# Weight gradient of a strided convolution: stored sums of the second batch's input rows, three more split leaves, and a new written order

## The chip, the cores and the metric

The kernel runs on one core of a Trainium2 chip. The metric is the time of the program on the device in microseconds (us). The engines are called by their short names in the profile: PE is TensorE with its matmuls, PEld its weight loads, DVE VectorE, ACT ScalarE, POOL GpSimd and SP SyncE, the engine from whose queue nearly all DMAs are issued. Engines run side by side, each works through its own instructions in the order written, and they wait for each other by semaphores.

## The reference

The reference is a convolution over time with 31 taps, stride 2 and 256 channels in and out, on two sequences (batches) of 16000 rows, then a normalisation over the whole time axis for each channel, scale and shift, and a tanh-approximated GELU. The function returns the output and the gradients to all four inputs.

```python
def _fwd_reference(x, w, gn_gamma, gn_beta):      # x (2,16000,256)  w (31,256,256), bfloat16
    s, L = 2, (T - K) // 2 + 1                    # L = 7985
    h = sum(einsum('blc,cd->bld', x[:, i:i + s*L:s, :], w[i]) for i in range(K))
    mu = h.sum(1) / L;  var = ((h - mu)**2).sum(1) / L
    return gelu((h - mu) / sqrt(var + 1e-5) * gn_gamma + gn_beta)
def reference(x, w, gn_gamma, gn_beta, grad_out):
    out, vjp = jax.vjp(_fwd_reference, x, w, gn_gamma, gn_beta)
    return (out, *vjp(grad_out))                  # out, dx, dw, dgamma, dbeta
```

## The kernel before, in words

The program has three large pieces of matmul work: the forward convolution (stages F0 and F1), the gradient to x (G0 for batch 0 up to its last chunk, G1 from there on), and the gradient to w (W). In all three a nested scheme of sums replaces four products by three: rows or taps are grouped in pairs, and a product of a pair is made from the three combinations "first", "second" and "both", called A, C_ and B_. In W the scheme has three levels. The outer two give nine combinations n = 0 to 8, listed in COMBOS as (i1, i2):

```python
COMBOS = ((A, A), (A, C_), (A, B_), (C_, B_), (B_, B_), (B_, A), (B_, C_), (C_, A), (C_, C_))
```

**A combination n of W.** weight_grad() goes through the nine of them. For each it needs two tiles of x rows per batch (`xt[b, 0]` and `xt[b, 1]`, 128 x 4096 elements, 1 MB each), their sum `XSUM[b]`, and rows of the incoming gradient, which the input gradient has left in DRAM as nine tensors dl_d per batch. Where B_ stands in a combination, the x tile is a sum of two raw tiles. x_tile (L1325) makes it: for batch 0 it loads a finished sum from the DRAM tensor xs_d; for batch 1 it loads two raw tiles and adds them on DVE with w_add (L1316). Where B_ stands in both places it adds two tiles that are there. XSUM is one more w_add for each batch (L1507), except for batch 0 in combinations 6 and 7, where it is loaded from xss_d.

Within a combination there are three products, worked in two halves h of 256 input channels and kept in PSUM pairs X[h] and Y[h]. The one of the sums (pm) goes first: pair_x (L1417 or L1421) and pair_d (L1437) make sums and differences on DVE, w_pairs multiplies them, w_single multiplies the singles. Then come leaf A into Y and leaf C_ into X, both on top of what pm left. A leaf is either whole (w_leaf: for each half and each batch 16 matmuls with 512 columns) or split once more, if (n, leaf) stands in NODES. A split leaf has pair_x, two pair_d, w_pairs with 16 matmuls of 256 columns for each half, w_both (L1461), which adds the kept product of pm to PSUM on DVE, and w_single with 32 matmuls of 256 columns for each half. So w_single waits for w_both, and w_both for w_pairs. leaf_d (L1520 for n = 0, L1525 after) makes the leaf's gradient rows DL. Results are kept by ACT (L585), added by DVE (L581), or added and sent out by w_emit (L1380).

```python
NODES = {(6, C_), (5, A), (0, A), (0, C_), (1, A), (2, A), (3, A), (4, A), (6, A), (7, A), (7, C_), (8, C_)}
```

**The stored sums of batch 0.** x_sums(f) (L750), called eight times in the forward pass of batch 0, loads 1 MB of raw rows into XA, makes the three sums with three adds on DVE (L754 twice, L758 once), and stores them to xs_d (two DMAs) and xss_d (one). Eight such calls cover a batch.

**The input gradient.** input_grad() goes over batch b, chunk c = 0 to 3, half chunk pr = 0 and 1, and the three branches br in the order B_, A, C_. One (b, c, pr) is called a turn here; it ends with a store of 1 MB to out_1 out of the tile HO. Results of branches A and C_ are put into HO by ACT (L585) and corrected by a DVE add (L1213), or, in chunks 0 to 2 of batch 0, by one DVE add (L1217). HO has two buffers of 8192 bytes per partition: chunks 0 to 2 of batch 0 use only HO[0], all later turns alternate with pr. ACT also copies shared products for TensorE (g_copy, L1165). dl_turn transposes gradient rows by DMA and POOL stores them to dl_d. The next chunk's gradient tiles are loaded by SP (e_load).

**Memory.** Nearly all tiles lie at fixed offsets in one arena per partition, and tiles of different stages overlap. HO[1] lies at bytes 144128 to 152320; the tiles DL of the stage W begin at 146880. HO[0] lies at 119232 to 127424, and a buffer for a split leaf of n = 0 at 110720 to 127104.

**Order.** Every operation is first put in a list with its reads and writes; an operation in it is one instruction, or for TensorE a group of usually 8 or 16 matmuls. The list SEQUENCE, a written permutation of the operations' numbers, then fixes the order in which all are emitted; each engine keeps that order, and SP's DMA queue too.

## Time and profile before

| | |
|---|---|
| timed runs | 1113.3, 1113.68 and 1115.04 us; median 1113.68 us |
| the profiled execution, first to last instruction | 1111.2 us (the page gives no other time of it) |
| PE busy | 1086.2 us, 98% |
| weight loads busy | 749.8 us, 67% |
| DVE busy | 919.9 us, 83% |
| ACT busy | 578.9 us, 52% |
| POOL busy | 129.3 us, 12% |
| DMA moved | 256.16 MB, mean 231 GB/s |

The stages follow each other on TensorE: forward until about 407 us, input gradient from there to about 801 us, weight gradient to 1106 us; the rest is the last store. A busy share over the whole span mixes these stages, so the stretches are looked at one by one. In a row of stretches each engine's busy time stands in us with its count of instructions in brackets; the DMA share is the time that packets took, over 16 DMA engines, and can pass 1. In a row of waits stand the total, the number of times and the longest.

### The profile page before, as it was taken

How to read it: one execution, taken by the hardware profiler on the slowest of the kernel's cores; microseconds unless marked ns; L12 is line 12 of the kernel's file. 1: busy time of each engine (PE TensorE's matmuls, PEld its weight loads, DVE VectorE, ACT ScalarE, POOL GpSimd, SP SyncE). 2: the span in 40 equal slices, each digit the busy share in tenths (PEclk: the TensorE clock that was granted, in tenths of full speed). 3: DMA queues.
4: the chain of work that ended last, by engine and by line, in shares of the span. 5: the costliest groups of instructions: out<-in, count | busy, mean ns of one | idle time of the engine just before them, and what ended most of it. 6: DMA issues, size and time to landing. Idle time of an engine off the chain costs nothing.

```text
span 1111.2 us, 18967 instructions
## 1 busy us (share of the span) xinstructions
PE 1086.2 (98%) x7623; PEld 749.8 (67%) x7672; DVE 919.9 (83%) x900; ACT 578.9 (52%) x880; POOL 129.3 (12%) x233
## 2 busy tenths in 40 slices
PE   6999999999999989999999999999999999999998
PEld 4888899878787974444444444444587776678885
DVE  7987877889999999989897565644789699699995
ACT  1234434587988569899964566545413322111221
POOL 0000000000001003232332432251200000000000
PEclk9999999999999999999999999999999999999999
DMA  9979899876969789999999898577994959978888
GB/s 231 198 188 249 233 275 267 219 167 162 209 166 219 240 328 270 274 252 265 217 225 237 179 203 183 157 201 197 278 293 137 270 156 298 303 254 279 282 253 207
DMA packets 348806, 256.16 MB, mean 231 GB/s; under 512 B 234327, under 2 KB 315869, under 8 KB 343517
## 3 DMA queue, kind: packets, MB, share of 16 engines
q1 hardware_dynamic: 341613, 236.05, 81.8%
q0 software_dynamic: 7104, 18.89, 6.3%
q8 instruction: 60, 0.98, 0.4%
q14 instruction: 29, 0.24, 0.1%
HBM read 114.62 MB, written 84.45 MB: 179 GB/s over the span
## 4 chain that ended last, share of the span: by engine, by line
PE 89%; DVE 5%; issue 2%; DMA 1%; SPq 1%; ACT 1%; DVEq 0%
PE ps L1136 34%; PE ps L506 34%; PE ps L1351 21%; SPq L314 1%; DMA out_dram<-arena 1%; DVE arena L1437 1%; DVE ps L1461 1%; DMA arena<-in_w_dram 1%; DVE arena L1421 1%; DVE arena L1380 1%; DVE arena L1525 0%; DVE arena L581 0%; DVE arena L1417 0%; DVE arena L448 0%; DVE arena L1316 0%
## 5 line engine op out<-in xcount | busy, mean ns | idle before, releaser
L506 PE MATMUL ps<-arena 128*128 128x256 bf16 (+4 forms) x3464 | 396.6, 278 | 11.2 <-DMA arena<-in_x_dram 4.7
L1136 PE MATMUL ps<-arena 128*128 128x512 bf16 (+1 forms) x1787 | 388.1, 376 | 5.7 <-ACT ps L1165 3.6
L506 PEld LDWEIGHTS <-arena 128*128 128x128 bf16 x3464 | 338.2, 98 | 69.4 <-DMA arena<-in_x_dram 5.8
L1136 PEld LDWEIGHTS <-arena 128*128 128x128 bf16 x1824 | 178.5, 98 | 215.1 <-issue 2.9
L1351 PE MATMUL ps<-arena 128*128 128x256 bf16 (+1 forms) x2372 | 301.6, 289 | 3.4 <-DVE arena L1520 1.8
L1351 PEld LDWEIGHTS <-arena 128*128 128x128 bf16 x2384 | 233.2, 98 | 71.9 <-issue 2.3
L585 ACT ACTIVATE arena<-ps 128x1024 bf16<-128x1024 f32 (+1 forms) x121 | 122.1, 1022 | 213.0 <-PE ps L1351 77.3
L464 DVE TENSOR_TENSOR arena<-arena 128x2064 bf16<-128x2064 bf16 (+7 forms) x131 | 162.7, 1265 | 24.2 <-PE ps L506 23.0
L314 POOL DMA_DIRECT2D dld<-arena x144 | 104.6, 728 | 246.7 <-DMA arena<-arena 229.4
L1199 DVE TENSOR_TENSOR ps<-ps,arena 128x1024 f32<-128x1024 f32 x36 | 44.3, 1232 | 64.2 <-PE ps L1136 53.2
L1082 DVE TENSOR_TENSOR arena<-arena 128x1032 bf16<-128x1032 bf16 (+1 forms) x114 | 89.5, 813 | 9.5 <-POOL arena L1049 4.3
L551 ACT ACTIVATE ps<-ps 128x256 f32<-128x256 f32 x89 | 36.7, 412 | 85.6 <-PE ps L506 84.5
L1316 DVE TENSOR_TENSOR arena<-arena 128x4096 bf16<-128x4096 bf16 x30 | 68.3, 2287 | 0.5 <-DMA arena<-in_x_dram 0.3
L1165 ACT COPY ps<-ps 128x512 f32<-128x512 f32 x84 | 48.1, 575 | 33.7 <-PE ps L1136 30.0
L323 POOL MEMSET arena<- 128x104 bf16 (+11 forms) x52 | 12.0, 249 | 414.8 <-DVE arena L464 157.6
L923 DVE TENSOR_TENSOR arena<-arena 128x2048 bf16<-128x2048 bf16 (+1 forms) x48 | 57.5, 1197 | 3.0 <-ACT arena L926 1.3
L605 ACT ACTIVATE arena<-ps 128x512 bf16<-128x512 f32 (+1 forms) x64 | 37.0, 582 | 32.7 <-PE ps L506 28.2
L885 DVE TENSOR_TENSOR arena<-arena 128x2048 bf16<-128x2048 bf16 (+1 forms) x40 | 47.7, 1197 | 4.0 <-ACT arena L879 1.7
L1437 DVE TENSOR_TENSOR arena<-arena 128x2048 bf16<-128x2048 bf16 x40 | 48.5, 1220 | 2.4 <-PE ps L1351 2.4
L1461 DVE TENSOR_TENSOR ps<-ps,arena 128x1024 f32<-128x1024 f32 x24 | 29.1, 1227 | 19.5 <-PE ps L1351 19.5
L1453 ACT COPY ps<-ps 128x256 f32<-128x256 f32 x54 | 19.0, 360 | 47.8 <-PE ps L1351 46.7
L1525 DVE TENSOR_TENSOR arena<-arena 128x4608 bf16<-128x4608 bf16 x16 | 40.6, 2554 | 0.0
(92 smaller groups left out, 752.3 us busy)
## 6 DMA issues: line engine op xcount, KB each, us to landing
arena<-in_x_dram SPq DMA_DIRECT2D x36, 1024.0 KB
arena<-hd SPq DMA_DIRECT2D x40, 512.0 KB
dld<-arena POOLq DMA_DIRECT2D x144, 128.0 KB, 4.4
out_dram<-arena SPq DMA_DIRECT2D x14, 1024.0 KB
arena<-dld SPq DMA_DIRECT2D x18, 640.0 KB
arena<-dld SPq DMA_DIRECT2D x18, 576.0 KB
vl<-arena SPq DMA_DIRECT2D x36, 256.0 KB
arena<-vl SPq DMA_DIRECT2D x9, 1024.0 KB
```

The lines of the kernel that those rows point to most:

```text
L314: lambda: e.dma_start(out=out, in_=in_), dma=np_ * ns / 16e3 * 1.03, ns=ns, tp=SH[pk], slack=slack)
L464: lambda: nc.vector.tensor_tensor(out=o, in0=a, in1=b, op=ALU.add))
L506: yield nc.tensor.matmul(ps[:, dh, cs], lhsT=wt, rhs=mv, start=s0, stop=False, skip_group_check=True)
L585: lambda: nc.scalar.activation(out=out, in_=ps, func=ACT.Copy, scale=scale))
L885: add("DVE", dve(nf), [o], [a, b_], lambda: V.tensor_tensor(out=o, in0=a, in1=b_, op=op))
L923: add("DVE", dve(nf), [o], [a, b_], lambda: V.tensor_tensor(out=o, in0=a, in1=b_, op=op))
L1082: lambda: nc.vector.tensor_tensor(out=o, in0=a, in1=b, op=ALU.subtract))
L1136: yield nc.tensor.matmul(ps[:, e, 0:wide], lhsT=lt, rhs=mv, start=s0, stop=False, skip_group_check=True)
L1165: add("ACT", act(512), [o], [i], lambda: nc.scalar.copy(out=o, in_=i))
L1316: add("DVE", dve(4096), [o], [a, b], lambda: nc.vector.tensor_tensor(out=o, in0=a, in1=b, op=ALU.add))
L1351: yield nc.tensor.matmul(ps[:, s, c0:c1], lhsT=lt, rhs=mv, start=s0, stop=False, skip_group_check=True)
L1437: add("DVE", dve(2048), [o], [u, v], lambda o=o, u=u, v=v: nc.vector.tensor_tensor(out=o, in0=u, in1=v, op=ALU.subtract))
```

## The change

The x sums are made for batch 1 as well. x_sums gets a batch argument, xs_d and xss_d get one tensor per batch, and the tile for batch 1's sums, XB, takes the memory of HO[1], so that HO has one buffer left. The eight calls for batch 1 stand in the input gradient at branch A of each turn of batch 1; in the new written order their operations lie between the last chunk of batch 0 and the last turn of batch 1. x_tile and XSUM load batch 1's sums as they do batch 0's. Leaf C_ of combinations 3, 4 and 5 is split (three more entries in NODES). The numbers of operations change with this (3357 before, 3423 after), and the whole of SEQUENCE is written anew.

```diff
 SEQUENCE = """
...
 """
...
-    xs_d = dram.tile([P, 8, 2, 3, 512], BF16, name="xsd")
-    xss_d = dram.tile([P, 8, 2, 512], BF16, name="xssd")
+    xs_d = [dram.tile([P, 8, 2, 3, 512], BF16, name=f"xsd{b}") for b in range(NB)]
+    xss_d = [dram.tile([P, 8, 2, 512], BF16, name=f"xssd{b}") for b in range(NB)]
...
-    def x_sums(f):
-        load(XA, xblk(0)[:, f].rearrange("p (k r) c -> p k r c", k=2), 1 << 20, 4096)
-        for o, v in ((XA[:, :, 1:4:2], XA[:, :, 0:4:2]), (XA[:, :, 0], None)):
-            u = XA[:, :, 2] if v is None else v
+    XB = sb(GREG + 16704, 2, 4, 512)
+
+    def x_sums(f, b=0):
+        xa = (XA, XB)[b]
+        load(xa, xblk(b)[:, f].rearrange("p (k r) c -> p k r c", k=2), 1 << 20, 4096)
+        for o, v in ((xa[:, :, 1:4:2], xa[:, :, 0:4:2]), (xa[:, :, 0], None)):
+            u = xa[:, :, 2] if v is None else v
             add("DVE", dve(o.free_size()), [o], [o, u], lambda o=o, u=u: nc.vector.tensor_tensor(out=o, in0=o, in1=u, op=ALU.add))
...
+        load(xs_d[b][:, f, :, 0:2], xa[:, :, 0:2], 1 << 19, 2048)
+        load(xs_d[b][:, f, :, 2], xa[:, :, 3], 1 << 18, 1024)
+        o, u = xa[:, 0, 1:3], xa[:, 1, 1:3]
+        add("DVE", dve(1024), [o], [o, u], lambda o=o, u=u: nc.vector.tensor_tensor(out=o, in0=o, in1=u, op=ALU.add))
+        load(xss_d[b][:, f], o, 1 << 18, 2048)
...
-        ho = HO[pr if both else 0]
+        ho = HO[0]
...
-    NODES = {..., (7, C_), (8, C_)}
+    NODES = {..., (7, C_), (8, C_), (4, C_), (5, C_), (3, C_)}
...
-            if b == 0 and B_ in (i1, i2):
-                load(t, xs_d[:, :, k3, {(C_, B_): 0, (B_, A): 2, (B_, C_): 1}[i1, i2]], 1 << 20, 1024)
+            if B_ in (i1, i2):
+                load(t, xs_d[b][:, :, k3, {(C_, B_): 0, (B_, A): 2, (B_, C_): 1}[i1, i2]], 1 << 20, 1024)
                 return t
...
-                if b == 0 and n in (6, 7):
-                    load(XSUM[b], xss_d[:, :, n - 6], 1 << 20, 1024)
+                if n in (6, 7):
+                    load(XSUM[b], xss_d[b][:, :, n - 6], 1 << 20, 1024)
                 else:
                     w_add(XSUM[b], xt[b, 0], xt[b, 1])
...
         if (pr, br) == (1, B_):
             dl_turn(b, c, leaf)
+        if b == 1 and br == A:
+            x_sums(2 * c + pr, 1)
```

More of the change, by code (lines that the diff above doesn't have):

```diff
@@ L748, in conv_stem_kernel @@
     XSTEPS = {0: (0, 1), 1: (2, 3, 4), 2: (5, 6, 7)}
-    def x_sums(f):
-        load(XA, xblk(0)[:, f].rearrange("p (k r) c -> p k r c", k=2), 1 << 20, 4096)
-        for o, v in ((XA[:, :, 1:4:2], XA[:, :, 0:4:2]), (XA[:, :, 0], None)):
-            u = XA[:, :, 2] if v is None else v
-            add("DVE", dve(o.free_size()), [o], [o, u], lambda o=o, u=u: nc.vector.tensor_tensor(out=o, in0=o, in1=u, op=ALU.add))
-        load(xs_d[:, f, :, 0:2], XA[:, :, 0:2], 1 << 19, 2048)
-        load(xs_d[:, f, :, 2], XA[:, :, 3], 1 << 18, 1024)
-        o, u = XA[:, 0, 1:3], XA[:, 1, 1:3]
-        add("DVE", dve(1024), [o], [o, u], lambda: nc.vector.tensor_tensor(out=o, in0=o, in1=u, op=ALU.add))
-        load(xss_d[:, f], o, 1 << 18, 2048)
+    XB = sb(GREG + 16704, 2, 4, 512)
[4 more added lines that the diff above has]
+            u = xa[:, :, 2] if v is None else v
+            add("DVE", dve(o.free_size()), [o], [o, u], lambda o=o, u=u: nc.vector.tensor_tensor(out=o, in0=o, in1=u, op=ALU.add))
+        load(xs_d[b][:, f, :, 0:2], xa[:, :, 0:2], 1 << 19, 2048)
[3 more added lines that the diff above has]
+        load(xss_d[b][:, f], o, 1 << 18, 2048)
     VR = sb(REG, 2, 2, 2, 512)
@@ L1306, in conv_stem_kernel @@
     LATE = {2: ((0, 202816),), 3: ((1, 202816),), 8: ((2, 24576), (3, 182144))}
-    NODES = {(6, C_), (5, A), (0, A), (0, C_), (1, A), (2, A), (3, A), (4, A), (6, A), (7, A), (7, C_), (8, C_)}
+    NODES = {(6, C_), (5, A), (0, A), (0, C_), (1, A), (2, A), (3, A), (4, A), (6, A), (7, A), (7, C_), (8, C_), (4, C_), (5, C_), (3, C_)}
     P1 = [sb(94336 + 4096 * i, 1024, dt=FP32) for i in range(8)]
```

213 rows, old and new, of the table SEQUENCE are left out of this document.

## The prediction

> **What bounds the kernel now.** I read the page's totals first, then its forty slices, its chain, and then the busy times of chosen stretches.
>
> ```profile
> span 1111.2 us, 18967 instructions
> PE 1086.2 (98%) x7623; PEld 749.8 (67%) x7672; DVE 919.9 (83%) x900; ACT 578.9 (52%) x880; POOL 129.3 (12%) x233
> ...
> PE   6999999999999989999999999999999999999998
> ...
> DVE  7987877889999999989897565644789699699995
> ...
> DMA  9979899876969789999999898577994959978888
> ...
> PE 89%; DVE 5%; issue 2%; DMA 1%; SPq 1%; ACT 1%; DVEq 0%
> ```
>
> TensorE (PE) is busy 98% of the span, and 89% of the chain that ended last is its work. The forty slices show it full from the second slice to the last; the places where it is not are the start and the change from the forward pass to the input gradient. So time can only be taken out by giving TensorE less to do, and every stage has to keep feeding it afterwards. VectorE (DVE) is the next engine, 83% over the whole span, but very unevenly:
>
> ```profile
> 100.00:200.00 100.00, 98.61 (x935) 91.21 (x933) 76.95 (x76) 45.68 (x108) 1.87 (x3) 1.00 0.97 253
> 400.00:500.00 100.00, 95.73 (x482) 47.72 (x490) 94.95 (x119) 89.31 (x121) 26.69 (x43) 1.00 1.03 276
> 500.00:600.00 100.00, 99.53 (x463) 46.07 (x471) 87.40 (x107) 77.58 (x96) 31.69 (x59) 1.00 0.97 233
> 590.00:790.00 200.00, 199.00 (x917) 91.56 (x935) 114.05 (x126) 112.80 (x147) 61.28 (x106) 1.00 0.82 196
> 813.90:1106.50 292.60, 290.95 (x2276) 223.66 (x2287) 264.27 (x179) 68.23 (x98) 2.69 (x4) 1.00 0.82 251
> 1011.70:1073.30 61.60, 60.60 (x554) 53.78 (x551) 61.26 (x48) 10.13 (x15) 0.00 (x0) 1.00 0.84 271
> ...
> 1080.00:1090.00 10.00, 9.95 (x65) 6.22 (x64) 9.04 (x8) 2.79 (x3) 0.53 (x1) 1.00 1.00 229
> 1090.00:1100.00 10.00, 9.95 (x62) 6.08 (x62) 5.34 (x5) 2.37 (x2) 0.00 (x0) 1.00 0.94 215
> 1100.00:1110.00 10.00, 6.50 (x54) 5.08 (x52) 4.44 (x5) 0.00 (x0) 0.00 (x0) 1.00 0.64 177
> ```
>
> Columns: stretch, its length, busy PE, weight loads, VectorE, ScalarE, GpSimd, clock, DMA share, GB/s. The granted clock is 1.00 throughout. From 590 to 790, the input gradient's part where the new sums go, VectorE works 114.05 of 200 us, so 86 us are free. In the weight gradient (813.9 to 1106.5) it works 264.27 of 292.6 us, and from 1011.7 to 1073.3 it works 61.26 of 61.60 us: there it is as full as TensorE. The chain of work says the same, it runs over VectorE alone there:
>
> ```profile
> 1013.78 1.22 DVE arena L1437
> ...
> 1072.11 1.14 DVE arena L1421
> 1073.30 10.87 PE ps L1351 x97
> ```
>
> So the weight gradient has two nearly equal bounds, and both must be counted.
>
> **The change, part by part.** *Leaf C of combinations 3, 4 and 5.* A whole leaf is 64 matmuls of 512 columns (two halves h, two batches, 16 each). Split, it is 32 matmuls of 256 columns in w_pairs and 64 in w_single, 96 in all. Prices:
>
> ```profile
> L1351 PE MATMUL ps<-arena 128*128 128x512 bf16 x49 | 10.7, 379 | 0.1
> ...
> L1351 PE MATMUL ps<-arena 128*128 128x256 bf16 x96 | 10.7, 273 | 1.0 <-DVE arena L1421 1.0
> ...
> L1351 PEld LDWEIGHTS <-arena 128*128 128x128 bf16 x2287 | 223.7, 98 | 70.6 <-issue 2.3 <-DVE arena L1421 1.5
> ```
>
> The first row is a stretch of 10.7 us with nothing but 512-column matmuls (49), the second one of 10.7 us with 96 of 256 columns and one other. That is 0.218 and 0.110 us each (the printed means overlap). A leaf goes from 64 x 0.218 = 14.0 us to 96 x 0.110 = 10.6 us, 3.4 us less, and three leaves give **-10.2 us** of TensorE work. The third row, 98 ns for a weight load, is still below the 110 ns of a 256-column matmul, so 32 more weight loads a leaf stay covered.
>
> The Trainium skill, "TensorE: Matmul & The Clock Gate", section "Back-to-back issue gap", says otherwise: in real streams of weight load and matmul the spacing is about 81 ns at 128 columns and 131 ns at 512, so a wide matmul gains more from overlap than a narrow one. An estimate from that page, taking 98 ns for 256 columns between the two, makes a whole leaf 8.4 us and a split one 9.4 us, three splits 3 us dearer, and the sum below +6.0 instead of -7.2 us (1119.7 us). The first row, 218 ns at 512 columns, speaks against it here.
>
> *What the splits ask of VectorE, and what the stored sums give back.*
>
> ```profile
> L1316 DVE TENSOR_TENSOR arena<-arena 128x4096 bf16<-128x4096 bf16 x28 | 63.7, 2288 | 0.5 <-DMA arena<-in_x_dram 0.3
> L1437 DVE TENSOR_TENSOR arena<-arena 128x2048 bf16<-128x2048 bf16 x40 | 48.5, 1220 | 2.4 <-PE ps L1351 2.4
> L1461 DVE TENSOR_TENSOR ps<-ps,arena 128x1024 f32<-128x1024 f32 x24 | 29.1, 1227 | 19.5 <-PE ps L1351 19.5
> L1421 DVE TENSOR_TENSOR arena<-arena 128x2048 bf16<-128x2048 bf16 x22 | 26.3, 1220 | 0.0
> L1417 DVE TENSOR_TENSOR arena<-arena 128x4096 bf16<-128x4096 bf16 x8 | 18.3, 2288 | 0.0
> ...
> L754 DVE TENSOR_TENSOR arena<-arena 128x2048 bf16<-128x2048 bf16 (+1 forms) x16 | 15.3, 955 | 1.7 <-DMA arena<-in_x_dram 1.4 <-issue 0.2
> L758 DVE TENSOR_TENSOR arena<-arena 128x1024 bf16<-128x1024 bf16 x8 | 5.5, 688 | 3.5 <-DMA xsd<-arena 3.5
> ```
>
> Each split needs pair_x (2.288 us at L1417 for combinations 3 and 5; two of 1.220 at L1421 for 4, whose tiles lie too far apart), two pair_d (1.220, L1437) and two w_both (1.227, L1461): 7.0 + 7.3 + 7.4 = 21.7 us in all. Removed are eight w_add of 4096 elements (L1316): six in x_tile for the second batch, two for XSUM in combinations 6 and 7: 8 x 2.288 = 18.3 us. VectorE in the weight gradient: +3.4 us, to 264.3 + 3.4 = 267.7 us.
>
> TensorE's need falls to 292.6 - 10.2 = 282.4 us. VectorE fits only if it idles no more than 282.4 - 267.7 = 14.7 us; it idled 28.3 us. Of these, 7.7 us lie behind 1080 us, where the three rows above give 18.8 of 26.5 us busy; the last leaf has little for it to do, and they stay. So idle time in the middle must fall from 20.6 to 7.0 us. What it was:
>
> ```profile
> DVE ps L1461 <- PE ps L1351: 19.5, 4, 9.9
> DVE arena L1380 <- PE ps L1351: 4.7, 3, 4.0
> DVE arena L1437 <- PE ps L1351: 2.4, 3, 1.3
> ...
> PE ps L1351 <- DVE arena L1520: 1.8, 1, 1.8
> PE ps L1351 <- DVE arena L1421: 1.0, 1, 1.0
> ```
>
> 19.5 us is w_both waiting for the w_pairs in front of it: VectorE was early. An engine that falls behind no longer waits like that. The bounds of this stage are therefore -10.2 us (idle time vanishes as needed) and +3.4 us (every idle microsecond remains). Between them I go by the nearest row, the stretch in which VectorE already led: it cost TensorE 61.60 - 60.60 = 1.0 us in 61.6 us. Counting the operations, at these durations, in the new written order between the first matmuls of combination 1 and of combination 8 gives VectorE 234 us against 227 us for TensorE (before: 232 against 239), so VectorE now leads for some 228 us: 228 / 61.6 x 1.0 = **+3.7 us**. Behind the added w_both in VectorE's queue stand the next combination's adds, and TensorE's w_single waits for it; the written order puts two or three matmul groups (1.8 us each) between w_pairs and that w_single, which covers 1.2 us but not a queue that runs 5 us late.
>
> *The sums of the second batch.* Eight times, from 590 to 790 us, two adds at L754 (15.3 us over eight) and one at L758 (5.5 us): 20.8 us into 86 us of free VectorE. Cost 0; without that cover it would be up to 20.8 us. Each time SP also issues a load of 1 MB and stores of 512, 256 and 256 KB, 32 issues, while the weight gradient loses twelve raw loads and gains eight: 28 issues more on SP and none on POOL. A store waits on SP for its add, and the transposes and out_1 stores behind it wait too. The twelve and eight are 1 MB each, so the last stage moves 4 MB less, and the input gradient 16.8 MB more. The eight loads go into the same tiles as the raw ones, with one landing to wait for instead of two landings and an add: 0.
>
> ```profile
> 820.00:830.00 10.00, 10.00 (x93) 8.90 (x92) 10.00 (x8) 0.10 (x1) 2.16 (x3) 1.00 1.08 364
> ...
> SPq L319 <- DMA dld<-arena: 40.4, 15, 7.2
> ```
>
> At the best rate of any stretch, 364 GB/s, 16.8 MB take 46 us of full DMA: the share goes from 0.82 to (164 + 46) / 200 = 1.05. The stretches from 400 to 600 us ran at 1.03 and 0.97 with TensorE at 99.5% in the second, and the first batch's sums ran at 0.97 from 100 to 200 us. So the sums themselves are hidden up to about this load; SP has 40.4 us of waits for buffers there, which bounds a delay through it from above. I take +0.5 us, between 0 and +10 (share 1.05 squeezed to 1.00).
>
> *HO.* Its second buffer becomes XB, so each turn's 1 MB of out_1 must be stored before the next turn's first evacuation. The last such store but one:
>
> ```profile
> 804.03 6.89 DMA out_dram<-arena
> ```
>
> 6.89 us plus 0.5 to issue. In the new order three of the turns leave only 24 matmuls of 512 columns, 5.2 us, between store and evacuation; the other turns leave more. Late by 2.2 us three times, 6.6 us at most, and on ScalarE the next turn's g_copy, which TensorE needs, stands behind the evacuation; the single-buffered turns of chunks 0 to 2 left 7.3 us and up and show no TensorE wait, and a second PSUM pair lies between. I take +0.5 us; the lower end is 0.
>
> *Into the weight gradient.* The 6.89 us store read HO's second buffer, on which the first DL tiles lie; leaf_d (L1520) waited for it and TensorE for leaf_d, 1.8 us. Now that memory is read by the last x sums' 256 KB stores, issued eight matmul groups before leaf_d, and the last out_1 store leaves memory that is written a dozen VectorE operations later. **-1.7 us**; bounds -1.8 and +2 (SP runs late there).
>
> *New order.* In forward and input gradient, groups on TensorE move by at most 13 places, and SP's weight loads at the start swap places. I take 0, with 1.5 us to either side, part of the 4.3 us that TensorE misses from 400 to 500 us.
>
> Sum: -10.2 + 3.7 + 0.5 + 0.5 - 1.7 = **-7.2 us** on the profiled span of 1111.2 us, 1104.0 us. The median of the timed runs, 1113.68 us, lies 2.5 us above that span (launch and end): **1106.5 us**. A measurement tells 0.2%, 2.2 us, from no change.
>
> **Rivals.** *VectorE feeds TensorE without loss.* Its waits vanish as they did from 1011.7 us on: -10.2 - 1.7 = -11.9, 1101.8 us. For it: 61.6 us at full load with 1.0 us lost. Against: that stretch lived on a lead built up before it.
>
> *VectorE becomes the bound.* If its idle time in the middle falls only to 15 to 20.6 us, the stage takes 290 to 296 us, -2.2 to +3.4; with the rest 1110.8 to 1116.4 us. The splits have then only moved the bound: the change does not do what it says. For it: in-order waits of up to 9.9 us for one w_both.
>
> *The input gradient becomes DMA-bound, the case on the other side.* At 820 to 830 us the share reaches 1.08, so it can pass 1; but if transposes (small packets) hold it at 1.00, 210 us of work take 210 us: +10, leaf buffers are freed late, TensorE waits. -7.2 + 10 - 0.5 = +2.3, 1116 us. It decides from about 7 us of backlog.
>
> *Weight loads set the pace.* If a matmul of either width took the 98 ns of a weight load, a split would add 32 x 0.098 = 3.1 us a leaf, +9.4 instead of -10.2: 1126 us. The 218 ns row nearly excludes it. The rule of the Trainium skill's page named above would be its reason.
>
> **How the numbers follow.** Forecast (1103.5 to 1110) 0.50; without loss 0.16; VectorE-bound 0.20; DMA-bound 0.11; weight loads 0.01; something unseen 0.02. Faster by over 0.2%: 0.48 + 0.16 + 0.07 + 0.02 = 0.73; within: 0.02 + 0.08 + 0.02 = 0.12; slower: 0.05 + 0.07 + 0.01 + 0.02 = 0.15. The range 1101.5 to 1115 leaves out part of the first rival (0.05) and most of the DMA-bound and slower cases (0.13).
>
> **What would show it.** Right: 96 more matmuls of the weight gradient and a stage of some 286 us, VectorE at 94% or more in it, waits of L1461 for PE below 10 us in all, no wait of L1520 for out_dram, VectorE near 135 us from 590 to 790 us, TensorE still at 99% there. Wrong: waits of PE on VectorE lines of several microseconds (VectorE-bound), or waits of PE for L1082 or L585 with a DMA share of 1.0 or more (DMA, HO).

## The result, and the profile after

The changed kernel takes 1189.12 us (median of four runs, 1185.75 to 1190.3) against 1113.72 us for the kernel before on the same chip: ratio 1.0672, 95% interval 1.0654 to 1.0689. It is 75 us slower; 7 us of gain were forecast. The profiled execution took 1190.3 us, its span is 1188.4 us. First the totals, the slices and the chain from the page of the kernel after:

```profile
span 1188.4 us, 19262 instructions
PE 1100.7 (93%) x7724; PEld 762.7 (64%) x7768; DVE 945.6 (80%) x932; ACT 581.4 (49%) x880; POOL 128.7 (11%) x233
...
PE   4999999899999999889889888899789999999997
...
DVE  4977877799899988789677837556358989999995
...
PEclk8999999999999999999999999999999999999999
DMA  9579898886888799988789988877798485687988
...
PE 18%; DVE 6%; DMA 3%; SPq 2%; issue 2%; ACT 0%; DVEq 0%; ACTq 0%
```

TensorE's busy time rose by 14.5 us (1086.2 to 1100.7), although the split leaves take matmul time away, and its idle time by 62.7 us (25.0 to 87.7). The idle tenths lie in the first slice, the eighth and those from 475 to 890 us; the last quarter is as full as before. The chain that ended last is of no help here: its shares add up to 31% of the span (99% before), its first piece is at 819 us, and so it does not reach back into the two pieces where the time is lost. The stretches that answer to those of before, with the same columns; lines of the code stand three to six lower in the kernel after (L506 is L509, L1136 is L1142, L1351 is L1357):

```profile
0.00:100.00 100.00, 79.06 (x639) 64.14 (x640) 74.63 (x72) 21.82 (x50) 2.24 (x13) 0.93 0.76 174
100.00:200.00 100.00, 97.05 (x902) 87.90 (x901) 76.45 (x76) 43.11 (x95) 1.48 (x2) 1.00 0.92 237
400.00:500.00 100.00, 93.70 (x593) 57.99 (x597) 89.10 (x110) 75.39 (x113) 14.18 (x27) 1.00 0.97 267
500.00:600.00 100.00, 87.68 (x387) 39.04 (x394) 79.10 (x87) 76.73 (x94) 29.01 (x56) 0.97 0.83 219
590.00:790.00 200.00, 179.43 (x789) 79.76 (x804) 127.56 (x157) 107.42 (x139) 56.50 (x93) 0.96 0.89 233
885.70:1182.30 296.60, 293.28 (x2461) 241.90 (x2468) 278.17 (x197) 73.64 (x106) 3.26 (x5) 0.99 0.78 241
```

The last row is the weight gradient: TensorE works 293.3 of 296.6 us, as full as the prediction wanted it. The loss is in the two pieces ahead of it. From 590 to 790 us TensorE works 179.4 us where it worked 199.0, at a DMA share of 0.89, below 1. The granted clock, 1.00 throughout before, is 0.93, 0.97 and 0.96 in the three of these rows in which TensorE works less than 90% of the time.

What TensorE waited for, the two longest groups of before and the six longest of after (total, times, longest):

```profile
PE ps L506 <- DMA arena<-in_x_dram: 4.7, 1, 4.7
PE ps L1136 <- ACT ps L1165: 3.6, 4, 1.1
```
```profile
PE ps L1142 <- DVE ps L1205: 16.0, 7, 5.2
PE ps L509 <- DVE arena L451: 11.7, 2, 9.8
PE ps L1142 <- ACT ps L1171: 10.7, 8, 2.3
PE ps L1142 <- DVE arena L1088: 6.9, 6, 2.9
PE ps L509 <- DVE ps L584: 6.9, 4, 2.3
PE ps L509 <- DMA arena<-in_x_dram: 5.3, 2, 4.6
```

No single wait carries it. It is many waits of at most about 5 us on VectorE and ScalarE, and one of 9.8 us at the start. Nearly every one of them stands in code that the diff of the functions does not touch.

All kernels are cut at the last matmul of the forward, input gradient and weight gradient lines, read from stretches of a quarter of a microsecond. (The expectations cut after's weight gradient at its first full stretch, 885.7 us: in after, 34 of its matmuls, 5.5 us, stand ahead of the last one of the input gradient; in before it is 2.) Lengths in us:

| kernel | median us | ratio to before, interval | forward | input gradient | weight gradient |
|---|---|---|---|---|---|
| before | 1113.7 | 1 | 408.0 | 393.8 | 304.8 |
| after | 1189.1 | 1.0672 [1.0654, 1.0689] | 433.2 | 457.0 | 292.2 |
| order_only | 1183.2 | 1.0619 [1.0591, 1.0647] | 435.5 | 433.2 | 312.8 |
| ops_only | 1247.5 | 1.1192 [1.1172, 1.1213] | 408.8 | 474.5 | 357.0 |
| fwd_old_order | 1180.3 | 1.0591 [1.0576, 1.0607] | 420.2 | 459.2 | 293.0 |
| splits_only | 1172.1 | 1.0532 [1.0513, 1.0550] | 408.0 | 393.8 | 359.8 |
| sp_order | 1273.2 | 1.1426 [1.1403, 1.1449] | 461.8 | 477.8 | 327.0 |
| eng_order | 1265.1 | 1.1353 [1.1330, 1.1376] | 489.0 | 463.0 | 306.2 |
| no_sums | 1166.4 | 1.0459 [1.0429, 1.0488] | 435.0 | 433.0 | 292.0 |
| no_sums_two_ho | 1173.5 | 1.0529 [1.0511, 1.0546] | 435.5 | 433.0 | 298.5 |
| start_new | 1124.5 | 1.0093 [1.0077, 1.0108] | 419.5 | 394.0 | 304.8 |
| sums_no_adds | 1190.3 | 1.0685 [1.0671, 1.0700] | 433.0 | 457.0 | 292.5 |
| sums_no_stores | 1177.9 | 1.0575 [1.0550, 1.0599] | 432.8 | 447.8 | 292.2 |
| sums_small | 1170.3 | 1.0511 [1.0496, 1.0525] | 434.5 | 437.0 | 292.2 |
| g_new | 1177.2 | 1.0569 [1.0550, 1.0589] | 414.0 | 437.2 | 319.2 |
| hybrid | 1172.2 | 1.0527 [1.0513, 1.0542] | 409.0 | 393.8 | 362.5 |
| one_split_4 | 1140.8 | 1.0243 [1.0229, 1.0258] | 408.8 | 393.8 | 332.2 |
| one_split_5 | 1138.1 | 1.0220 [1.0203, 1.0238] | 408.0 | 393.8 | 330.5 |
| jitter_4 | 1273.5 | 1.1435 [1.1402, 1.1468] | 479.5 | 479.5 | 308.5 |
| jitter_16 | 1725.7 | 1.5495 [1.5450, 1.5540] | 695.8 | 716.2 | 307.8 |

The 75 us are +25.2 in the forward pass, +63.2 in the input gradient and -12.6 in the weight gradient; of the last figure 5.5 us are the matmuls that now stand ahead of the cut.

### The profile page after: what moved, and what is told of

It is laid out like the page before. It is cut to its first block, busy times and chain, and to the rows that moved or that the text cites. A ratio compares the mean times of both kernels' runs of the same rounds, so it can differ in the third digit from the quotient of the medians.

```text
span 1188.4 us, 19262 instructions
## 1 busy us (share of the span) xinstructions
PE 1100.7 (93%) x7724; PEld 762.7 (64%) x7768; DVE 945.6 (80%) x932; ACT 581.4 (49%) x880; POOL 128.7 (11%) x233
## 5 line engine op out<-in xcount | busy, mean ns | idle before, releaser
L1142 PE MATMUL ps<-arena 128*128 128x512 bf16 (+1 forms) x1786 | 404.0, 383 | 45.4 <-DVE ps L1205 16.0
L509 PE MATMUL ps<-arena 128*128 128x256 bf16 (+4 forms) x3464 | 402.9, 280 | 30.2 <-DVE arena L451 11.7
L509 PEld LDWEIGHTS <-arena 128*128 128x128 bf16 x3464 | 339.6, 99 | 93.2 <-issue 14.7
L1142 PEld LDWEIGHTS <-arena 128*128 128x128 bf16 x1824 | 180.1, 99 | 268.6 <-issue 59.2
L1357 PE MATMUL ps<-arena 128*128 128x256 bf16 (+1 forms) x2474 | 294.5, 282 | 6.1 <-DVE arena L1427 3.0
L1357 PEld LDWEIGHTS <-arena 128*128 128x128 bf16 x2480 | 243.0, 98 | 57.5 <-DVE arena L1427 4.0
L588 ACT ACTIVATE arena<-ps 128x1024 bf16<-128x1024 f32 (+1 forms) x121 | 121.6, 1021 | 249.2 <-PE ps L1357 95.3
L467 DVE TENSOR_TENSOR arena<-arena 128x2064 bf16<-128x2064 bf16 (+8 forms) x131 | 162.6, 1265 | 31.6 <-DMA arena<-in_x_dram 17.6
L1205 DVE TENSOR_TENSOR ps<-ps,arena 128x1024 f32<-128x1024 f32 x36 | 43.9, 1229 | 36.3 <-PE ps L1142 31.0
L929 DVE TENSOR_TENSOR arena<-arena 128x2048 bf16<-128x2048 bf16 (+1 forms) x48 | 57.6, 1199 | 14.6 <-ACT arena L932 8.2
L608 ACT ACTIVATE arena<-ps 128x512 bf16<-128x512 f32 (+1 forms) x64 | 36.8, 580 | 44.8 <-PE ps L509 29.6
L326 POOL MEMSET arena<- 128x78 bf16 (+11 forms) x52 | 11.3, 234 | 428.5 <-DVE arena L467 156.0
L1322 DVE TENSOR_TENSOR arena<-arena 128x4096 bf16<-128x4096 bf16 x22 | 50.1, 2286 | 9.4 <-DMA arena<-in_x_dram 5.5
L1443 DVE TENSOR_TENSOR arena<-arena 128x2048 bf16<-128x2048 bf16 x46 | 55.1, 1218 | 1.8 <-DMA arena<-arena 1.7
L891 DVE TENSOR_TENSOR arena<-arena 128x2048 bf16<-128x2048 bf16 (+1 forms) x40 | 47.8, 1198 | 7.0 <-ACT arena L883 4.5
L760 DVE TENSOR_TENSOR arena<-arena 128x2048 bf16<-128x2048 bf16 (+1 forms) x32 | 30.6, 955 | 27.6 <-DMA arena<-in_x_dram 26.4
L970 ACT ACTIVATE arena<-arena,stats 128x1024 bf16<-128x1024 bf16 x16 | 19.2, 1235 | 49.3 <-DMA arena<-hd 28.3
L1467 DVE TENSOR_TENSOR ps<-ps,arena 128x1024 f32<-128x1024 f32 x30 | 36.1, 1225 | 7.5 <-PE ps L1357 7.4
```

What stands on the lines that cost most here:

```text
L467: lambda: nc.vector.tensor_tensor(out=o, in0=a, in1=b, op=ALU.add))
L509: yield nc.tensor.matmul(ps[:, dh, cs], lhsT=wt, rhs=mv, start=s0, stop=False, skip_group_check=True)
L588: lambda: nc.scalar.activation(out=out, in_=ps, func=ACT.Copy, scale=scale))
L929: add("DVE", dve(nf), [o], [a, b_], lambda: V.tensor_tensor(out=o, in0=a, in1=b_, op=op))
L1142: yield nc.tensor.matmul(ps[:, e, 0:wide], lhsT=lt, rhs=mv, start=s0, stop=False, skip_group_check=True)
L1322: add("DVE", dve(4096), [o], [a, b], lambda: nc.vector.tensor_tensor(out=o, in0=a, in1=b, op=ALU.add))
```

## The experiments

To build an order for other operations than it was written for, the matmul groups that both kernels have serve as a scale: an operation taken from the other order goes to the same place between the same groups, and moves behind what it depends on where that is needed.

**The order alone, and the operations alone.**

```diff
# order_only: before.py
-SEQUENCE = <order of before>
+SEQUENCE = <forward pass and input gradient: order of after; weight gradient: order of before>
# ops_only: after.py
-SEQUENCE = <order of after>
+SEQUENCE = <order of before, new operations at their place between the groups of after>
# fwd_old_order: after.py
+SEQUENCE = <forward pass: order of before; all else: order of after>
```

> The operations of the kernel before (no sums of batch 1, two buffers HO, no new split leaves); those of the forward pass and of the input gradient stand in the order of the kernel after, those of the weight gradient in the order of the kernel before. In the kernel after the forward pass ended 25 us later and the input gradient took 58 us more than before. Theory 1 (the written order alone makes both): forward to about 433 us, input gradient about 450 us, weight gradient 305 us, about 1190 us. Theory 2 (the order makes the 25 us of the forward pass, the DMAs of the new sums the 58 us of the input gradient): forward to 433 us, input gradient 394 us, about 1139 us. Theory 3 (the single buffer HO makes the 58 us): as theory 2, 1139 us. Neither the order at all: 1114 us.

> The operations of the kernel after (sums of batch 1, one buffer HO, three more split leaves), those that the kernel before has too in the order that they have there, the new ones at the place that they have in the kernel after between the same matmul groups. Theory 1 (the written order alone makes the loss): forward to 408 us, input gradient 394 to 396 us, weight gradient about 297 us, 1104 to 1107 us, faster than before. Theory 2 (the DMAs of the new sums make the 58 us of the input gradient): forward to 408 us, input gradient about 450 us, about 1165 us. Theory 3 (the single buffer HO): the same as theory 2, about 1165 us, but then with ACT waiting in L588 for stores where theory 2 has waits on loads and transposes.

> The kernel after with the operations of the forward pass alone in the order of the kernel before. All theories that put the forward loss on the order: forward to 408 us (433 in the kernel after), the rest as in the kernel after, about 1164 us. If the 25 us have another cause, or come back as waits in the input gradient: about 1189 us. If what the input gradient loses comes from work that the forward pass left late: well below 1164 us.

order_only: 1183.2 us, with none of the change's operations. The forward pass loses 27.5 us and the input gradient 39.4 us (and the weight gradient 8.0 us at the seam of the two orders); theory 1 holds for most of the loss. Its second half, that the operations of after would be fast in the order of before, is false: ops_only takes 1247.5 us. Its forward pass takes 408.8 us, so the forward loss is the order's alone. In the input gradient it is slower than after (474.5 against 457.0 us): the change's operations can't stay in the order of before either. The single HO is a cost there (the first row is ScalarE's waiting from 408 to 884 us, the others are TensorE's):

```profile
ACT arena L588 <- DMA out_dram<-arena: 55.1, 7, 15.0
PE ps L1142 <- ACT arena L588: 42.2, 9, 9.5
PE ps L1357 <- DVE arena L1443: 18.8, 4, 10.8
PE ps L1357 <- ACT arena L588: 15.9, 3, 11.7
```

TensorE waits 42.2 us in the input gradient for ScalarE's evacuations (L588) into HO, which wait 55.1 us for stores of earlier turns; the order of before was written for two buffers. And the weight gradient takes 357 us, of which more below. fwd_old_order, expected near 1164 us, takes 1180.3. It gives back 13 us of the forward pass's 25; the rest is lost at the end of the forward pass, at the seam of the two orders, where the operations of the input gradient begin: from 380 to 420 us TensorE works 30.4 us, against 36.8 us in before, and up to 380 us as much as there. The input gradient gains nothing by it (459.2 us), so its loss is not the forward pass's lateness handed on.

**The start.**

```diff
# start_new: before.py; the same 160 operations first, in another order among themselves
-SEQUENCE = <operations 1 to 160 as before> ...
+SEQUENCE = <operations 1 to 160 as they follow each other in after> ...
```

> The kernel before with its first 160 operations put in the order that they have among each other in the kernel after (144 of the 160 move, four far SP stores stay); everything from operation 161 on as before. It covers the first 60 us or so. If the start's order makes its own loss by VectorE waiting for a transpose with the weight sums of L448 that TensorE needs queued behind (9.8 us of TensorE's waiting at 17 to 27 us in the kernel after), and the later order as before can't give it back: TensorE waits 9 to 10 us for L448 and the run takes 1114 + 10 to 13 = 1124 to 1127 us. If the start's lateness is multiplied, since the whole later order then meets transfers and copies at other times: over 1130 us. If it is made up for, since only TensorE's sum of work counts: 1114 us is excluded as TensorE was 98% busy.

1124.5 us: +10.7, as the first theory has it, and the later stages are not changed by it (394.0 and 304.8 us). VectorE's instructions in this stretch, of before and of start_new (start, length, line, operation, count, idle time before it and what ended it):

```profile
12.10 2.99 DVE L464 TENSOR_TENSOR arena<-arena 128x1040 bf16<-128x1040 bf16 x3
15.01 7.02 DVE L448 TENSOR_TENSOR arena<-arena 128x2048 bf16<-128x2048 bf16 x6
22.26 2.48 DVE L448 TENSOR_TENSOR arena<-arena 128x2048 bf16<-128x2048 bf16 x2 [0.24 <-DMA arena<-in_w_dram]
```
```profile
13.34 0.68 DVE L448 TENSOR_TENSOR arena<-arena 128x1024 bf16<-128x1024 bf16 x1
23.02 2.40 DVE L464 TENSOR_TENSOR arena<-arena 128x2080 bf16<-128x2080 bf16 x2 [9.00 <-DMA arena<-in_x_dram]
25.33 5.88 DVE L448 TENSOR_TENSOR arena<-arena 128x2048 bf16<-128x2048 bf16 x5
```
```profile
PE ps L506 <- DVE arena L448: 10.3, 2, 8.5
```

In before VectorE makes the row sums (L464) at 12 us and goes straight on to the weight sums (L448). In the new order two row sums stand behind two transposes of x rows. They wait 9.0 us for these to land, the weight sums stand behind them in VectorE's queue, and TensorE waits for these, once for 8.5 us. The row sums need none of the data that these transposes bring: by its reads and writes the list of operations names no dependence between them. They read two planes, and the transposes fill others that lie between these; that the compiled program waits because the spans of the accesses overlap is argued from the addresses, and was not tried by itself.

**The order of one queue, and of the input gradient.**

```diff
# sp_order: before.py
+SEQUENCE = <SP's operations of forward and input gradient: order of after; all others: order of before>
# eng_order: before.py
+SEQUENCE = <all but SP's operations there: order of after; SP's: order of before>
# g_new: before.py
+SEQUENCE = <operations of the input gradient in the order of after, in the places that they hold>
```

> The operations of the kernel before. SP's operations of the forward pass and the input gradient, the DMAs and transposes of its queue, stand in the order of the kernel after; all operations of the other engines, and the weight gradient, in the order of the kernel before. The run order_only, with all engines' operations of these two pieces in the new order, took 1183 us: forward 27 us and input gradient 37 us over before. Theory Q (the order of SP's queue makes the loss: transposes stand behind large transfers): at least 1165 us, with TensorE's long waits at the same places as in order_only. Theory E (the orders of VectorE and ScalarE make it: what TensorE needs stands behind an instruction that waits): 1114 to 1125 us.

> The reverse: the operations of the kernel before, the engines' operations of the forward pass and the input gradient in the order of the kernel after, those of SP's queue, and the weight gradient, in the order of the kernel before. Theory Q: 1114 to 1125 us. Theory E: at least 1165 us. Were it the combination of both (the engines' order of the kernel after expects transfers that the other queue's order brings later), both of these runs would be slow.

> The operations of the kernel before; only those of the input gradient (1487 of its 1495, eight far moved stores stay) are put, in the places that they hold, into the order that they have among each other in the kernel after. Forward pass and weight gradient as before (12 operations shift to keep dependences). order_only, with the forward pass in the new order too, lost 27 us there and 37 us in the input gradient. If the 37 us belong to the input gradient's own order: 1140 to 1155 us. If they were the late forward pass handed on (the GELU gradient's rows, on the chain of waits of order_only from 444 to 513 us, come too late): 1114 to 1122 us.

Both halves are slow, slower than the whole new order (1273.2 and 1265.1 against 1183.2 us). So neither queue's order alone is the flaw; the two belong to each other, the third case of the expectation. g_new, 1177.2 us and above all that was expected of it, shows that the input gradient's new order costs 43 us by itself (437.2 against 393.8), with 6 us more in the forward pass and 14 us at the seam to the weight gradient, where TensorE waits once for L1520 for 16.9 us. What the chain runs over in order_only (start, us, what; some of the pieces from 453 to 564 us):

```profile
453.65 1.84 ACT arena L926
455.52 1.24 DVE arena L923
...
482.61 1.23 ACT arena L916
...
499.23 6.37 DMA arena<-hd
...
546.83 7.21 DMA dld<-arena
554.05 1.20 SPq L319
555.31 2.45 DMA arena<-arena
```

TensorE hardly appears. ScalarE and VectorE make the gradient through the GELU (L916, L926, L923), a load brings its rows (hd), and POOL's store to dld with the transpose behind it on SP turns them; TensorE gets its rows as they come. In before 89% of the chain is TensorE's work, so these steps were hidden there. Which moved operations make the input gradient's chain late was not traced: no run moves some of them back alone, as start_new does for the start.

**How near another order may be.**

```diff
# jitter_16, jitter_4: before.py; forward pass and input gradient
+place of each operation + normal(0, 16) or normal(0, 4), dependences kept
```

> The operations of the kernel before; in the forward pass and the input gradient the place of each operation in the written order is shifted at random (normally distributed, 16 places of the 2756 there; dependences kept, weight gradient as before). Among VectorE's operations 1.44 pairs per operation change places, among TensorE's groups 1.32; in the order of the kernel after it is 2.64 and 1.41. order_only and g_new show what that order costs with the same operations: 69 and 64 us. If the order of the kernel after has a particular flaw, and an order in general bears such shifts: under 30 us, below 1145 us. If the order before fits this chip's times so closely that any other of that distance loses: 60 us or more, over 1174 us; well over it, if the new order, for its distance, is a planned and not a random one.

> The same with 4 places (about 0.35 changed pairs per operation). If the loss goes with the number of changed pairs: a quarter of what jitter_16 loses. If small shifts are covered by the slack that the order has: under 5 us, about 1115 to 1119 us.

+612 us and +160 us. In each the dearer of the cases named came out: jitter_16 is well over 60 us, and jitter_4 loses about a quarter of what jitter_16 loses (153 us), as its quarter of the changed pairs says. Four places of random shift cost more than twice what the whole change costs. Each is one random order; neither holds the time of before. That of after, with more changed pairs on VectorE than either, loses 67 us over these two pieces: for its distance it is well made. A near order need not be that dear: start_new costs 10.7 us.

**The sums of batch 1, and HO.**

```diff
# no_sums: after.py
-            x_sums(2 * c + pr, 1)
-                load(t, xs_d[b][:, :, k3, ...
+                load(t, xs_d[0][:, :, k3, ...
# no_sums_two_ho: no_sums and
-        ho = HO[0]
+        ho = HO[pr if both else 0]
# sums_no_adds: the three adds of x_sums for b == 0 only
# sums_no_stores: the three stores of x_sums for b == 0 only
# sums_small: sums_no_adds and
-        load(xa, xblk(b)[:, f] ...
+        load(xa[0:8], xblk(b)[0:8, f] ...      (the stores likewise)
```

> The kernel after in its own order, without the sums of batch 1 in the input gradient (8 loads of 1 MB, 24 additions, 24 stores are left out); the weight gradient loads batch 0's stored sums in the place of batch 1's, as many bytes. HO stays single. In the kernel after the input gradient took 452 us, in order_only, without the sums and with two buffers HO, 430 us. If the sums' transfers and additions make these 22 us: input gradient 430 us, about 1167 us. If the single buffer HO makes them: about 1187 us. If the order alone sets the input gradient: 1185 to 1189 us too, and the next run as well.

> As no_sums (sums of batch 1 left out, batch 0's loaded in their place), and HO has its two buffers as in the kernel before. If the single buffer costs what ScalarE and VectorE waited for its stores in the kernel after, 11.8 and 3.2 us: 10 to 15 us less than no_sums. If the stores were done in time anyway: the same as no_sums within 3 us.

> The kernel after in its own order, with the 24 additions of the sums of batch 1 on VectorE left out; their 8 loads and 24 stores stay (the stores write raw rows), and the weight gradient loads batch 0's sums in their place. The sums as a whole cost 22.8 us (kernel after 1189.1 less no_sums 1166.4). If the additions are it (VectorE, which works in order, waits in L760 and L764 for the load and the stores, 19.8 and 14.1 us in the kernel after): about 1167 us. If the transfers are it (they stand in SP's queue in front of transposes and loads): about 1186 us. If both are needed: in between.

> The kernel after in its own order, with the 24 stores of the sums of batch 1 left out (8 MB); the 8 loads of 1 MB and the 24 additions stay, and the weight gradient loads batch 0's sums. If VectorE's waiting for the loads is the cost: 1180 to 1189 us, with the waits in L760 for the load still there and those in L764 for the stores gone. If the stores in SP's queue are: about 1170 us.

> sums_no_adds with the 8 loads and 24 stores of the sums of batch 1 cut to 8 of 128 partitions each (16 times fewer bytes, 1 MB in all in the place of 16 MB, the same 32 DMAs in the same places of SP's queue); the additions are left out and the weight gradient loads batch 0's sums. The transfers as a whole cost 23 us (sums_no_adds 1190.3, no_sums 1166.4). If each DMA of SP holds one of the places in flight and what counts is how many stand in the queue: about 1185 to 1190 us. If what counts is how long such a place is held, or the bytes through the DMA engines: about 1167 us.

The sums cost 22.7 us (1189.1 less 1166.4), all in the input gradient: 457.0 against 433.0 us, which is what order_only takes there without any of the change. The adds cost nothing (1190.3). Without the stores 11.2 us of it are gone (1177.9, between the two cases expected), and cut to a sixteenth of their bytes the same 32 DMAs cost 3.9 us more than none: 20 of 24 us go by the size of the transfers, not by their number. Size has two ways to act, and these runs don't tell them apart: the bytes through the DMA engines, and the time for which SP's queue waits for such a transfer (from 590 to 870 us SP waits 13.4 us for loads and stores of the sums in after, 6.6 us in sums_small, none in no_sums). The same 230 us by the clock, though not quite the same work, in after and in no_sums:

```profile
640.00:870.00 230.00, 206.02 (x913) 91.91 (x931) 130.37 (x150) 111.68 (x147) 58.51 (x101) 0.97 0.86 229
```
```profile
640.00:870.00 230.00, 221.80 (x1029) 103.67 (x1049) 128.32 (x142) 120.80 (x160) 65.32 (x113) 0.99 0.76 201
```

With the sums the DMA share is 0.86 and TensorE works 206.0 us; without them 0.76 and 221.8 us. The DMA engines were not full on the mean in either. What grows is the landing time on the chain of the row turns; POOL's stores from 640 to 800 us (KB each, median us to landing), in after and in no_sums:

```profile
dld<-arena POOLq DMA_DIRECT2D x56, 128.0 KB, 5.2
```
```profile
dld<-arena POOLq DMA_DIRECT2D x56, 128.0 KB, 4.0
```

The median of 56 such stores is 1.2 us longer. That this is the way the transfers reach TensorE is argued; that their size is the cost is shown.

HO: without the sums, two buffers give the same 433.0 us in the input gradient, so in its own order the single buffer costs nothing there. The run is 7.1 us slower all the same, all of it in the weight gradient (298.5 against 292.0 us), where TensorE waits for the DL tiles that lie on HO's second buffer:

```profile
PE ps L1355 <- DVE arena L1524: 6.0, 2, 5.8
```

**The split leaves.**

```diff
# splits_only, hybrid: before.py
-    NODES = {..., (8, C_)}
+    NODES = {..., (8, C_), (4, C_), (5, C_), (3, C_)}
# splits_only: new operations put into the order of before
# hybrid: order of before, but that of after in the weight gradient
# one_split_4, one_split_5: only (4, C_), only (5, C_), put into the order of before
```

> The kernel before with the three more split leaves and nothing else (raw rows of batch 1 loaded and added in the weight gradient as before; HO with two buffers), in the order of the kernel before. If the split is worth what TensorE's rows give, 10.2 us less matmul time, and VectorE has room: about 1103.5 us. If VectorE, which has 264.3 us of work in the weight gradient before, is the bound with the new pair sums added and the additions of batch 1 still there: between 1108 us and no gain, 1114 us, with TensorE's waits for the pair sums grown.

> The kernel before with three more split leaves (no sums of batch 1, two buffers HO); forward pass and input gradient in the order of the kernel before, the weight gradient in the order of the kernel after, with the raw loads and additions of batch 1 put in at the place they have in the kernel before. splits_only, with the new operations put into the order of the kernel before, lost 54 us in the weight gradient, which took 359 us. If that loss was the fit of the order to the operations: weight gradient 298 to 304 us, in all 1107 to 1113 us. If VectorE is the bound, with the split leaves' sums and the additions of batch 1 both there: 310 to 325 us, in all 1119 to 1134 us. If neither order carries these operations: over 340 us.

> The kernel before with one more split leaf, C_ of combination 4, where VectorE has the most idle time (936 to 970 us: 25 us stretches of 21.5 and 20.0 us busy), new operations at their place in the kernel after, all else in the order of the kernel before. TensorE's work falls by 3.4 us, VectorE's grows by 7.3 us. If the idle time takes it: 1110 to 1111 us, faster than before. If in-order VectorE delivers the pair sums late: 1114 to 1125 us, with TensorE's waits on L1438 or L1422 grown. splits_only, with three, lost 54 us there.

> The same with leaf C_ of combination 5 alone, where VectorE is nearly full (975 to 1025 us: 23.97 and 24.71 of 25 us). If VectorE's local load decides: slower than one_split_4, 1117 to 1125 us. If only the fit of the written order decides: as one_split_4.

Without the stored sums the splits lose in every order that was tried: 1172.1, 1172.2, 1140.8 and 1138.1 us. With them they lose too in the order of before (ops_only, 357.0 us for the weight gradient). Neither of the two ways named for hybrid came out, it was the third. VectorE's local load doesn't decide either: one_split_4, where VectorE had 8.5 us free in 50, loses as much (27 us) as one_split_5 (25 us), where it was full. Where one_split_5 loses, TensorE and VectorE take turns. TensorE first (start, us, count, idle time before and its releaser), then VectorE, then the stretch as a whole:

```profile
1010.12 7.91 PE L1352 MATMUL ps<-arena 128*128 128x256 bf16 x48 [8.03 <-DVE arena L1438]
1021.20 5.32 PE L1352 MATMUL ps<-arena 128*128 128x256 bf16 x32 [3.17 <-DVE arena L1438]
```
```profile
1016.32 1.23 DVE L1438 TENSOR_TENSOR arena<-arena 128x2048 bf16<-128x2048 bf16 x1 [6.25 <-PE ps L1352]
...
1026.56 1.23 DVE L1438 TENSOR_TENSOR arena<-arena 128x2048 bf16<-128x2048 bf16 x1 [5.41 <-PE ps L1352]
```
```profile
1000.00:1025.00 25.00, 13.80 (x90) 10.47 (x88) 14.87 (x10) 1.02 (x1) 0.00 (x0) 0.74 0.27 79
```

pair_d (L1438) waits 6.25 us for TensorE, then TensorE 3.17 us for pair_d, then pair_d 5.41 us for TensorE. The code offers a reason: place() hands out the tiles for the pair sums in rotation, and for combinations 3 and 5 it has one tile only. The added leaf's pair_d can only write once the singles of the leaf before have read the tile, and the call added shifts the rotation, so that the next combination's first tile is the same one again: pair_d can't run ahead. In after the splits have the same tiles, but an order made for them, and less on VectorE (278.2 us in 296.6; 294.9 us in splits_only). A split with a tile of its own was not tried, so this reason is argued.

It is not the only one. Without the stored sums VectorE adds raw rows (L1317), and these additions can wait for their loads: 0.5 us in all in before, 4.2 us in one_split_4, and far longer in splits_only and in hybrid. What stands behind them in VectorE's queue waits too. Their rows in splits_only and in hybrid:

```profile
DVE arena L1317 <- DMA arena<-in_x_dram: 15.0, 2, 9.2
```
```profile
DVE arena L1317 <- DMA arena<-in_x_dram: 25.0, 4, 12.1
```

What each of the two reasons costs is open.

## Why the prediction was wrong

It said 1106.5 us, faster with 0.73, slower with 0.15, and something unseen with 0.02; the result lies 74 us above the top of its range. Step by step:

*The step that failed: "New order".* It was taken as 0 with 1.5 us to either side. order_only shows +27.5 and +39.4 us in the forward pass and the input gradient with unchanged operations, 67 us for a term put at 0. The working looked at TensorE's groups (at most 13 places moved) and at SP's first loads. It did not look at VectorE, where, counted in the two lists, 2.64 pairs of operations per operation change places (five small operations that move farther than 50 places left out), nor at what each moved operation would wait for. At the start this was to be read: two row sums stand behind transposes in the new list and before them in the old one, and weight sums that TensorE needs stand behind the row sums. For the rest of the 67 us it stays open which moves make them.

*The sums' transfers, +0.5 with bounds 0 and +10*: 22.7 us, over the upper bound. The bound came from a share of 1.05 squeezed to 1.00, that is, from bandwidth alone. They cost 24 us of the input gradient at a mean share of 0.86. The sum of bytes was right (16.8 MB); the reading that bytes are hidden up to a share of 1 was wrong. The rows on which it rested were of other stretches in another order, and even the new order, in which these transfers have their written places, doesn't hide them. The rival "DMA-bound" had the right place and sign, a price of 10 instead of 23 us, and a chance of 0.11.

*The sums' adds, 0*: right (sums_no_adds, 1190.3 against 1189.1 us). VectorE's busy time from 590 to 790 us is 127.6 us; 135 were forecast, for a kernel that had come farther by then.

*HO, +0.5 with 0 to 6.6*: right in the order of after, as far as the runs without the sums show (433.0 and 433.0 us). In the order of before it costs more than the upper end (42.2 us of waits, ops_only): the price belongs to an order, not to the buffer.

*Into the weight gradient, -1.7*: right in sign and mechanism; no wait of that line is left in after, and giving the second buffer back cost 6.5 us in no_sums_two_ho.

*The split leaves, -10.2, and VectorE's lateness, +3.7.* Right in sign, and the sum somewhat too large. The table's 304.8 to 292.2 us depends on the cut; what doesn't is TensorE's time on the lines of this stage, work and the idle time ahead of it: 301.6 + 3.4 us before, 294.5 + 6.1 us after (rows below), 4.4 us less, where the terms -10.2, +3.7 and -1.7 together said 8.2 us less. The matmuls fell by 7.1 us, not 10.2, at a clock of 0.99 instead of 1.00. The idle time rose by 2.7 us although 1.8 us for L1520 went, so the other waits grew by 4.5 us, not 3.7, and 2.2 us of them are for ScalarE (L588). The signs that the prediction named for this stage hold: w_both waits for TensorE 7.4 us in all (under 10), and VectorE works 278.2 of 296.6 us, 94%. Its sign for the input gradient failed: TensorE at 99% from 590 to 790 us, where it works 179.4 of 200 us.

```profile
L1467 DVE TENSOR_TENSOR ps<-ps,arena 128x1024 f32<-128x1024 f32 x30 | 36.1, 1225 | 7.5 <-PE ps L1357 7.4
```

The Trainium skill, "TensorE: Matmul & The Clock Gate", section "Back-to-back issue gap", states 131 ns a matmul at 512 columns in a real stream; by the prediction's estimate from it the splits would have cost TensorE time. Here 96 more and narrower matmuls took 7.1 us less.

*What was left out: the clock.* Some idle time is paid for again in slower matmuls behind it. The matmuls by line, of before and of after (busy, mean ns, idle time ahead):

```profile
L506 PE MATMUL ps<-arena 128*128 128x256 bf16 (+4 forms) x3464 | 396.6, 278 | 11.2 <-DMA arena<-in_x_dram 4.7
L1136 PE MATMUL ps<-arena 128*128 128x512 bf16 (+1 forms) x1787 | 388.1, 376 | 5.7 <-ACT ps L1165 3.6
L1351 PE MATMUL ps<-arena 128*128 128x256 bf16 (+1 forms) x2372 | 301.6, 289 | 3.4 <-DVE arena L1520 1.8
```
```profile
L509 PE MATMUL ps<-arena 128*128 128x256 bf16 (+4 forms) x3464 | 402.9, 280 | 30.2 <-DVE arena L451 11.7
L1142 PE MATMUL ps<-arena 128*128 128x512 bf16 (+1 forms) x1786 | 404.0, 383 | 45.4 <-DVE ps L1205 16.0
L1357 PE MATMUL ps<-arena 128*128 128x256 bf16 (+1 forms) x2474 | 294.5, 282 | 6.1 <-DVE arena L1427 3.0
```

The forward pass's matmuls are the same 3464 and took 402.9 us instead of 396.6; the input gradient's took 404.0 instead of 388.1. These 22 us are not waits. In after, up to its last matmul, the granted clock stands at 0.50 in nine stretches of 3.4 to 10.2 us. The first of them, and the sum of a row for each:

```profile
22.40:32.60 10.20, 5.67 (x20) 2.96 (x21) 10.17 (x10) 0.00 (x0) 0.00 (x0) 0.50 0.80 109
...
sum 40.20, PE 32.41 PEld 14.66 DVE 30.07 ACT 13.66 POOL 3.94; mean PE 3.60 PEld 1.63 DVE 3.34 ACT 1.52 POOL 0.44
```

TensorE works 32.4 us in them at half its clock. Without the last stretch, whose 3.3 us are the weight gradient's, that makes about 15 of the 22 us; what makes the rest is not shown. Not every wait costs this: in before the clock stays at 1.00 with 11.2 and 5.7 us of idle time ahead of the same lines. In the stretch of one_split_5 shown above 90 matmuls, mostly of 256 columns (0.110 us each in the prediction's rows), took 13.8 us, 0.153 us each, at a mean granted clock of 0.74. The Trainium skill, "TensorE: Matmul & The Clock Gate", section "What's actually happening", states that the array falls to half its clock after an idle window of some 3.4 us and needs a busy one to return. These rows agree: the clock is at 0.50 there, for 3.4 us at the shortest.

In all, by the stages of the table: order +67, sums +23, HO 0, weight gradient -13, together +77 of 75 us measured. The split of order and sums comes from one kernel each (order_only, no_sums), and they agree, since both leave 433 us in the input gradient. It holds for this way of taking the change apart. In the order of before the change's operations cost 80.7 us in the input gradient (ops_only, 474.5 against 393.8), and the new order takes 17.5 us off that.

## What to carry to other kernels

Where engines work in order through a list written out in full, that list is the kernel: changing it is the largest edit in the diff, and it has to be costed engine by engine, by what each moved instruction would wait for and by what stands behind it, not by how far TensorE's groups move. A gain that needs a new order (a split leaf, stored sums) is to be tried against the old order kept as far as it goes, and an order from a planner has to be timed before its operations are judged. A mean DMA share below 1 is no proof that transfers are hidden.

## What the runs showed of the hardware

Not expected: a random shift of four places in a list of 2756 operations costs 160 us of 800 (jitter_4), with no change in the work, and one of sixteen places 612 us, about four times as much for four times as many changed pairs. A DMA share below 1 is no free capacity: 16 MB of transfers cost 23 us in a piece whose share they raised from 0.76 to 0.86 (640 to 870 us), by their size and not by their number (sums_small, 1170.3 us). And 11 us without a matmul on TensorE in 25 us went with a mean granted clock of 0.74 in these 25 us (one_split_5); in after, 63 us of added idle time on TensorE came with 22 us of slower matmuls, about 15 of them in stretches at a clock of 0.50.
